# Two banks for the transposed weights, both heads' weights-times-v in one two-bank tile, and a new order of a pair's steps

## The chip, the cores and the metric

The kernel runs on one core of one Trainium2 chip. The metric is device microseconds from start to end of the program. TensorE (PE) does the matrix products and the transposes, VectorE (DVE), ScalarE (ACT) and GpSimd (POOL) the elementwise work, and the SP queue issues the transfers.

## The reference, cut to what matters

B = 2, H = 8, S = 576, D = 64. For each of the 16 heads a causal attention is mixed with a read-out of a memory, and the result (1152 tokens x 512) goes through two dense layers.

```
scores = scale * q @ k.T ; causal mask ; a = softmax(scores) ; local = a @ v
q_p = phi(q)                                  # elu(q) + 1
mem_out = (q_p @ M_prev) / (q_p @ z_prev + 1e-6)
x = g * mem_out + (1 - g) * local             # g from beta, one per head
h = ((x @ w1) * (x @ w2)) @ w3 ; x2 = h @ w_out
out = sum over 4 experts of p_e * (relu(x2 @ w1[e]) @ w2[e])
```

## The kernel before, in words

All products are taken in single precision; a value is split into a high and a low part where a product is done in three passes (`PASSES`).

**Slots.** The two heads of a pair share the 128 partitions. There are 8 pairs, and a loop of nine slots (n = -1 to 7, `run_slot`, L338). Slot n holds, for pair n, stage b (transposes of the weights, products with v, memory read-out, joining, `stage_b`, L242); for pair n+1, phi and stage a (scores and exponentials, L198); for pair n+2, the split of q and k (`stage_h`, L158). Besides this come "fill" steps that belong to the dense layers: folding w3 and w_out into one matrix W in slots 0 to 3 (L394), the a and b products of the first batch in slots 4 to 6.4 (L446), and the product with W from 6.4 to 8 (L507). Each step has a number between 0 and 1, its place in the slot (`H_AT`, `PHI_AT`, `A_AT`, `B_AT`, and `B_STEP` = 0.48 added for the odd head); the fill steps are spread evenly; the program writes all of them down in the order of these numbers. After slot 7 come the second batch and the four experts.

**Order on the engines.** The framework's planner takes the written order as priority, and lets an instruction of lower priority go first on an engine where by its model the one before it is not ready. The resulting order of each engine is fixed before the run: every engine takes its instructions in that order and waits at the head of its queue.

**Stage b before.** A head's 15 blocks of weights are transposed in groups of 4, 4, 4 and 3 (`trans`, L254) into the one bank of `psT`, and ACT copies each group to the tile pT in SBUF (L263). A product with v (`pv`, L266) goes into the one bank of `psQ`, head by head. `mem` (L279) takes one of the two two-bank tiles of `psS` for both heads. `join` (L303) divides a head's result on DVE (L306, L309, L311) and adds the memory part on POOL (L312). `fin` (L314) transposes the pair's result (L325) into a `psS` tile, whence ACT and DVE write xT (L328, L82). The scores of stage a (L212) also use the `psS` tiles, four times a pair. With `psM` (two banks) all eight banks are in use: 2 + 4 + 1 + 1.

In slot n the even head's steps lie at 0.02 to 0.42 and the odd head's at 0.50 to 0.90, in turn with the fill steps: transposes, then products with v that need their copies, then more transposes.

Of the kernel before, what the change touches and what calls it, by code (L numbers as in the profile page):

```python
# [8 lines left out]
F32 = mybir.dt.float32  # L9
# [4 lines left out]
ALU = mybir.AluOpType  # L14
AX = mybir.AxisListType
PSUM = bass.MemoryType.PSUM


H_AT = (0.6, 0.7, 0.62, 0.72)
PHI_AT = (0.3, 0.4)  # L20
A_AT = (0.25, 0.34, 0.43, 0.52)
B_AT = (0.02, 0.07, 0.1, 0.12, 0.15, 0.17, 0.22, 0.27, 0.32, 0.34, 0.42)
B_STEP = 0.48

WO_SLOTS = (-0.9, -0.8, -0.7, -0.6, -0.3, -0.1, 0.1, 0.2)
W_SLOTS, B_SLOTS, C_SLOTS = (0.0, 4.0), (4.0, 6.4), (6.4, 8.0)
# [7 lines left out]
def kernel(  # L34
# [17 lines left out]
    nc = tc.nc  # L52
    B, H, D, S = qT.shape
# [4 lines left out]
    P = 128  # L58
    KD = DM // P
    KF = DF // P  # L60
    NQ = 5
    RP = 120
# [9 lines left out]
    def r32(ap):  # L72
        return ap.bitcast(F32)
# [7 lines left out]
    def lo_dve(dst, src, hi):  # L81
        nc.vector.tensor_sub(dst, src, r32(hi))  # L82

    main = ctx.enter_context(tc.tile_pool(name="main", bufs=1, side="left"))
    gm = main.tile([P, H], F32, name="gm")
    gl = main.tile([P, H], F32, name="gl")
# [6 lines left out]
    def from64(raw, tmp, nm):  # L93
# [21 lines left out]
    attn = ExitStack()  # L115
    A1 = attn.enter_context(tc.tile_pool(name="A1", bufs=1, side="right"))
    A2 = attn.enter_context(tc.tile_pool(name="A2", bufs=2, side="right"))
# [7 lines left out]
        out=mask[:, S0:], in_=mask[:, S0:], compare_op=ALU.is_ge, fill=-MASK,  # L125
        base=0, pattern=[[-1, RP]], channel_multiplier=1,
    )
    psS = attn.enter_context(tc.tile_pool(name="psS", bufs=2, space=PSUM))
    psQ = attn.enter_context(tc.tile_pool(name="psQ", bufs=1, space=PSUM))
    psT = attn.enter_context(tc.tile_pool(name="psT", bufs=1, space=PSUM))  # L130


    raw_t, qk_t, phi_t, prob_t, xq_t, xm_t = {}, {}, {}, {}, {}, {}

    mz = A1.tile([P, B * H // 2, D + 1], F32, name="mz")

    v4 = [A1.tile([RP, NQ, D + 1], F32, name=f"v{i}") for i in range(4)]
# [20 lines left out]
    def stage_h(p):  # L158

        if p >= B * H // 2:  # L160
            return []
        qd, kd = raw_t[p]
        qk_t[p] = [A1.tile([P, 2, S], F32R, tag=f"{x}s", name=f"{x}s{p}") for x in "qk"]
        qs, ks = qk_t[p]
        return [
            *zip(
                H_AT,
                (
                    lambda: nc.scalar.copy(qs[:, 0, :], qd),
                    lambda: nc.scalar.copy(ks[:, 0, :], kd),  # L170
                    lambda: lo_pool(qs[:, 1, :], qd, qs[:, 0, :]),
                    lambda: lo_pool(ks[:, 1, :], kd, ks[:, 0, :]),
                ),
            )
        ]

    def stage_phi(p):
# [13 lines left out]

        return [*zip(PHI_AT, (f0, f1))]

    q0 = [R * i for i in range(NQ)]
    widths = [x + RP for x in q0]
    rows = [R] * (NQ - 1) + [RP]

    def stage_a(p):  # L198
# [37 lines left out]
        )  # L236
        return [(at, lambda c=c: scores(*c)) for at, c in zip(A_AT, steps)]

    NB = 4
    blocks = [(i, j) for i in range(NQ) for j in range(i + 1)]  # L240

    def stage_b(n):  # L242


        b, h = divmod(n, H)
        p, o = n // 2, n % 2 * D
        Pt, vn, phi = prob_t.pop(n), v4[n % 4], phi_t[p]
        st = {}
        pt = {}
        if n % 2 == 0:  # L250
            xq_t[0] = A2.tile([RP, NQ, 2, D], F32, tag="xq", name=f"xq{p}")
        xq = xq_t[0]

        def trans(g):  # L254
            def f():
                mine = blocks[g * NB : (g + 1) * NB]
                ps = psT.tile([P, 512], F32, tag="T", name=f"pt{g}_{n}")[0:RP, 0 : RP * len(mine)]
                t = A2.tile([RP, RP * len(mine)], F32, tag=f"pt{g}", name=f"pT{g}_{n}")
                for x, (i, j) in enumerate(mine):
                    sl = slice(x * RP, (x + 1) * RP)  # L260
                    nc.tensor.transpose(ps[:, sl], Pt[i][:, q0[j] : q0[j] + RP], identF[0:RP, 0:RP])  # L261
                    pt[i, j] = t[:, sl]
                nc.scalar.copy(t, ps)  # L263
            return f

        def pv(*tiles):  # L266
            def f():
                if "a" not in st:
                    ps = psQ.tile([P, 512], F32, tag="Q", name=f"a{n}")[0:RP, 0 : NQ * (D + 1)]
                    st["a"] = ps.rearrange("p (i d) -> p i d", d=D + 1)  # L270
                for i in tiles:
                    for j in range(i + 1):
                        nc.tensor.matmul(  # L273
                            st["a"][:, i, :], lhsT=pt[i, j][0 : rows[j]], rhs=vn[0 : rows[j], j, :],
                            start=(j == 0), stop=(j == i),
                        )
            return f

        def mem():  # L279
            if n % 2 == 1:  # L280
                return
            ps = psS.tile([P, 2, 512], F32, tag="S", name=f"b{p}")[0:RP, :, 0 : NQ * (D + 1)]
            m = ps.rearrange("p x (i d) -> p x i d", d=D + 1)
            for i in range(NQ):
                for x in range(2):
                    o = slice(x * D, (x + 1) * D)
                    nc.tensor.matmul(
                        m[:, x, i, :], lhsT=phi[o, q0[i] : q0[i] + RP], rhs=mz[o, p, :], start=True, stop=True
                    )
            r2 = A2.tile([RP, 2, NQ], F32, tag="rm", name=f"rm{p}")  # L290
            for x in range(2):
                nc.vector.tensor_scalar(
                    out=r2[:, x, :], in0=m[:, x, :, D], scalar1=1e-6, scalar2=gm[0:RP, h + x : h + x + 1],
                    op0=ALU.add, op1=ALU.mult,
                )
            nc.vector.reciprocal(r2, r2)
            xm_t[0] = dst = A2.tile([RP, 2, NQ, D], F32, tag="xm", name=f"xm{p}", bufs=1)
            for x in range(2):
                nc.vector.tensor_mul(
                    dst[:, x], m[:, x, :, 0:D], r2[:, x, :].unsqueeze(2).to_broadcast([RP, NQ, D])  # L300
                )

        def join():  # L303
            a = st["a"]
            rr = A2.tile([RP, NQ], F32, tag="rr", name=f"rr{n}")
            nc.vector.tensor_scalar(  # L306
                out=rr, in0=a[:, :, D], scalar1=1e-9, scalar2=gl[0:RP, h : h + 1], op0=ALU.add, op1=ALU.mult
            )
            nc.vector.reciprocal(rr, rr)  # L309
            xh = xq[:, :, n % 2, :]  # L310
            nc.vector.tensor_mul(xh, a[:, :, 0:D], rr.unsqueeze(2).to_broadcast([RP, NQ, D]))  # L311
            nc.gpsimd.tensor_add(xh, xh, xm_t[0][:, n % 2])  # L312

        def fin():  # L314
            if n % 2 == 0:
                return
            if b:
                xT[b, h // 2] = main.tile([P, 2, S], F32R, tag=f"g{p}", name=f"xT{b}_{h // 2}")
            xt = xT[b, h // 2]

            o0 = 512 - q0[NQ - 1]
            ps = psS.tile([P, 1024], F32, tag="S", name=f"x{p}")[:, o0 : o0 + S]
            for c in range(NQ):
                w = rows[c]
                nc.tensor.transpose(  # L325
                    ps[:, q0[c] : q0[c] + w], xq[0:w, c].rearrange("p h d -> p (h d)"), identF[0:w, 0:w]
                )
            nc.scalar.copy(xt[:, 0, :], ps)  # L328
            lo_dve(xt[:, 1, :], ps, xt[:, 0, :])

        return [
            *zip(
                [x + n % 2 * B_STEP for x in B_AT],
                (trans(0), trans(1), mem, trans(2), pv(0, 1), trans(3), pv(2), pv(3), pv(4), join, fin),
            )
        ]

    def run_slot(n, fill):  # L338
        steps = stage_h(n + 2) + stage_phi(n + 1) + stage_a(n + 1)
        steps += stage_b(2 * n) + stage_b(2 * n + 1) if n >= 0 else []  # L340
        steps += [((i + 0.5) / len(fill), f) for i, f in enumerate(fill)]
        for _, f in sorted(steps, key=lambda t: t[0]):
            f()
# [260 lines left out]
    for e in range(E):  # L604
        nxt = None
        for c, (c0, cw) in enumerate(CHUNKS):
            hs = []
            for m in range(KF):
                ps = ps3.tile([P, 512], F32, tag="P", name=f"d{e}_{c}_{m}")[:, 0:cw]
                n = 0  # L610
                for kk in range(KD):
                    rhs = x2a[kk][:, :, c0 : c0 + cw] if c0 < CA else x2b[kk][:, :, c0 - CA : c0 - CA + cw]
                    for wi, xi in PASSES:
                        nc.tensor.matmul(  # L614
                            ps, lhsT=ew1[m // 4 * 4 + kk][:, wi, m % 4 * P : (m % 4 + 1) * P],
                            rhs=rhs[:, xi, :], start=(n == 0), stop=(n == 3 * KD - 1),
# [5 lines left out]
                    out=ht[:, 1, :], in0=ps, scalar=0.0, in1=r32(ht[:, 0, :]),  # L622
                    op0=ALU.max, op1=ALU.subtract,
                )
                hs.append(ht)
            for tt in range(cw // P):
                po = ps3.tile([P, 512], F32, tag="P", name=f"o{e}_{c}_{tt}")
                n = 0
                for kk in range(KF):
                    for xi, wi in PASSES:  # L630
                        nc.tensor.matmul(  # L631
                            po, lhsT=hs[kk][:, xi, tt * P : (tt + 1) * P], rhs=ew2[kk][:, wi, :],
# [55 lines left out]
```

## Time and profile before

| | |
|---|---|
| three runs | 790.2, 799.09 and 799.87 us; median 799.09 us |
| the profiled execution | 802.59 us, its span 800.8 us, so 1.8 us lie around the span |
| busy: PE, DVE, ACT, POOL | 760.1 us (95%), 305.3 (38%), 255.5 (32%), 249.2 (31%) |
| mean granted TensorE clock | 0.972 |
| attention and fill (slots) | from 0 to about 312 us; the second batch and the experts follow |

A row of the chronological view gives the start, the duration, the engine, the source line, the operation, the tile written and the tiles read, how many instructions are merged in the row, and in brackets how long the engine stood idle before it and what ended that. A product with v and one of mem count as two PE instructions in the trace, a transpose as one. A granted clock of 1.00 is 2.4 GHz, 0.50 is 1.2 GHz.

### The profile page before, as it was taken

To read this page: it belongs to the slowest core of one execution; us is meant where nothing else is said; L and a number is where in the kernel's file an instruction comes from. 1 tells how busy PE (TensorE), PEld (TensorE's weight loads), DVE (VectorE), ACT (ScalarE), POOL (GpSimd) and SP (SyncE) were. 2 spreads that over 40 slices of the span, in tenths; PEclk is the share of its full clock that TensorE was granted. 3 is DMA by queue.
4 is the path that set the end of the run, shared out by engine and by line. 5 is a ranking of instruction groups with operands and counts; after the bars stand their busy time and mean duration, and the time that the engine had idled before them with its cause. 6 is when DMAs were issued, how large, how long until landed. Compare 5 with 4: busy or idle time off the path is not lost.

```text
span 800.8 us, 11325 instructions
## 1 busy us (share of the span) xinstructions
PE 760.1 (95%) x4568; PEld 671.9 (84%) x4568; DVE 305.3 (38%) x650; ACT 255.5 (32%) x503; POOL 249.2 (31%) x252
## 2 busy tenths in 40 slices
PE   4889999899999998899999999999999999999998
PEld 2668778799988898889988988889888898888986
DVE  7965574537676421655331211212112121121211
ACT  7855564636565522455220101201012010120100
POOL 2253544215453103923392009500085001600000
PEclk9989999859999998999999999999999999999999
DMA  9753303302423001541141004200033000201010
GB/s 270 270 170 102 117 17 91 91 19 79 141 84 114 28 1 53 158 145 54 29 131 53 0 1 121 90 1 0 1 118 94 1 0 1 67 1 39 14 40 27
DMA packets 52596, 56.69 MB, mean 71 GB/s; under 512 B 15552, under 2 KB 40128, under 8 KB 52544
## 3 DMA queue, kind: packets, MB, share of 16 engines
q1 hardware_dynamic: 52544, 55.97, 23.2%
q8 instruction: 36, 0.59, 0.3%
q14 instruction: 16, 0.13, 0.1%
HBM read 53.60 MB, written 2.36 MB: 70 GB/s over the span
## 4 chain that ended last, share of the span: by engine, by line
PE 58%; POOL 3%; issue 2%; DMA 1%; DVE 1%; ACT 1%; POOLq 0%; SPq 0%; DVEq 0%; ACTq 0%
PE d L614 25%; PE o L631 25%; PE c L507 4%; PE ab L446 3%; POOL el L79 1%; DMA wr<-in_moe_w_dram 1%; POOL ws L79 1%; POOL el L76 1%; PE a L273 1%; PE pt L261 0%; ACT tu L101 0%; POOL xq L312 0%; DVE P L224 0%; DVE tu L103 0%; PE x L325 0%
## 5 line engine op out<-in xcount | busy, mean ns | idle before, releaser
L631 PE MATMUL o<-el,he 128*128 128x512 f32 x864 | 201.3, 393 | 0.0
L631 PEld LDWEIGHTS o<-el,he 128*128 128x128 f32 x864 | 161.8, 188 | 36.5
L620 ACT ACTIVATE he<-d 128x512 fp32r<-128x512 f32 (+2 forms) x96 | 47.2, 491 | 342.4 <-PE d L614 339.9
L446 PE MATMUL ab<-xT,ws 128*128 128x288 f32 x768 | 120.7, 309 | 4.1 <-DVE asb L494 1.7
L446 PEld LDWEIGHTS ab<-xT,ws 128*128 128x128 f32 x768 | 110.0, 197 | 7.8 <-issue 2.9
L614 PE MATMUL d<-x2b,el 128*128 128x384 f32 (+1 forms) x768 | 113.7, 308 | 0.0
L614 PEld LDWEIGHTS d<-x2b,el 128*128 128x128 f32 x768 | 113.1, 189 | 0.7
L621 DVE SCALAR_TENSOR_TENSOR he<-d,he 128x512 fp32r<-128x512 f32 (+2 forms) x96 | 53.6, 558 | 147.8 <-ACT he L620 147.8
L76 POOL TENSOR_SCALAR el<-rel 128x512 fp32r<-128x512 f32 x64 | 40.4, 637 | 213.7 <-PE d L614 186.2
L614 PE MATMUL d<-x2a,el 128*128 128x512 f32 x384 | 89.6, 394 | 0.0
L614 PEld LDWEIGHTS d<-x2a,el 128*128 128x128 f32 x384 | 72.0, 188 | 16.8
L79 POOL TENSOR_TENSOR el<-rel,el 128x512 fp32r<-128x512 f32 x64 | 83.6, 1322 | 1.6
L640 DVE SCALAR_TENSOR_TENSOR acc<-o,pr,acc 128x512 f32<-128x512 f32 x27 | 20.3, 751 | 125.7 <-PE o L631 125.7
L273 PE MATMUL a<-v,pT 114*120 114x65 f32 (+1 forms) x480 | 66.4, 284 | 0.1
L273 PEld LDWEIGHTS a<-v,pT 114*120 114x120 f32 (+1 forms) x480 | 63.8, 206 | 2.4 <-ACT tu_l L101 0.7
L507 PE MATMUL c<-hT,W 128*128 128x288 f32 x384 | 58.5, 300 | 3.3 <-DVE hT L82 3.0
L394 PE MATMUL wacc<-wo,w3s 128*128 128x512 f32 x192 | 56.0, 442 | 3.0 <-DVE W L82 2.4
L507 PEld LDWEIGHTS c<-hT,W 128*128 128x128 f32 x384 | 52.3, 188 | 5.6 <-DVE hT L82 3.1
L79 POOL TENSOR_TENSOR ws<-tf,ws 128x512 fp32r<-128x512 f32 x32 | 43.3, 1354 | 40.5 <-ACT ws L436 35.5
L261 PE MATMUL pt<-identF,P 120*120 120x120 f32 x240 | 41.3, 295 | 11.7 <-ACT pT L263 9.8
L394 PEld LDWEIGHTS wacc<-wo,w3s 128*128 128x128 f32 x192 | 39.6, 214 | 12.5 <-issue 3.3
L218 PE MATMUL sc<-ks,qs 64*120 64x120 f32 (+5 forms) x288 | 36.8, 381 | 12.4 <-POOL ks L79 8.6
(75 smaller groups left out, 654.8 us busy)
## 6 DMA issues: line engine op xcount, KB each, us to landing
wr<-in_moe_w_dram SPq DMA_DIRECT2D x32, 512.0 KB, 3.6
rel<-in_moe_w_dram SPq DMA_DIRECT2D x64, 256.0 KB, 2.7
w3r<-in_moe_w3T_dram SPq DMA_DIRECT2D x16, 512.0 KB, 3.7
wor<-in_moe_w_out_dram SPq DMA_DIRECT2D x8, 512.0 KB, 7.0
v<-in_v_dram SPq DMA_DIRECT2D x16, 150.0 KB, 3.9
qd<-in_qT_dram SPq DMA_DIRECT2D x8, 288.0 KB, 4.1
kd<-in_kT_dram SPq DMA_DIRECT2D x8, 288.0 KB, 3.9
out_dram<-acc SPq DMA_DIRECT2D x9, 256.0 KB, 2.0
```

What stands on the lines that cost most here:

```text
L76: nc.gpsimd.tensor_scalar(out=dst, in0=src, scalar1=1.0, scalar2=1.0, op0=ALU.mult, op1=ALU.mult)
L79: nc.gpsimd.tensor_sub(dst, src, r32(hi))
L218: nc.tensor.matmul(ps[x][:, c : c + k1 - k0], lhsT=qs[o, a, q0[i] : q0[i] + RP], rhs=ks[o, b, k0:k1], start=(m == 0), stop=(m == 2),)
L261: nc.tensor.transpose(ps[:, sl], Pt[i][:, q0[j] : q0[j] + RP], identF[0:RP, 0:RP])
L273: nc.tensor.matmul(st["a"][:, i, :], lhsT=pt[i, j][0 : rows[j]], rhs=vn[0 : rows[j], j, :], start=(j == 0), stop=(j == i),)
L394: nc.tensor.matmul(wacc[t], lhsT=w3s[u][:, a, c, :], rhs=wo[4 * g + c][:, bb, :], start=(g == 0 and c == 0 and x == 0), stop=(g == 1 and c ...
L446: nc.tensor.matmul(ps[:, 0:HS], lhsT=self.ws[u][:, wi, kk, :], rhs=xT[b, kk][:, xi, a * HS : (a + 1) * HS], start=(n == 0), stop=(n == 3 * ...
L507: nc.tensor.matmul(st["ps"][:, 0:HS], lhsT=Wt[kk][:, wi, d * P : (d + 1) * P], rhs=hT[kk][:, xi, a * HS : (a + 1) * HS], start=(kk == 0 an ...
L614: nc.tensor.matmul(ps, lhsT=ew1[m // 4 * 4 + kk][:, wi, m % 4 * P : (m % 4 + 1) * P], rhs=rhs[:, xi, :], start=(n == 0), stop=(n == 3 * KD ...
L620: nc.scalar.activation(ht[:, 0, :], ps, AF.Relu)
L621: nc.vector.scalar_tensor_tensor(out=ht[:, 1, :], in0=ps, scalar=0.0, in1=r32(ht[:, 0, :]), op0=ALU.max, op1=ALU.subtract,)
L631: nc.tensor.matmul(po, lhsT=hs[kk][:, xi, tt * P : (tt + 1) * P], rhs=ew2[kk][:, wi, :], start=(n == 0), stop=(n == 3 * KF - 1),)
```

## The change

`psQ` is dropped and `psT` gets two banks. `stage_b` is called once per pair. The eight groups of transposes (four per head) are written at 0.01 to 0.29 (`T_AT`); the products with v of head 0 at 0.40 and of head 1 at 0.48 go into the two banks of one `psS` tile; `join` at 0.54 divides both heads (two divisors, one reciprocal, two products on DVE) and adds the memory part in one POOL instruction of twice the length; `fin` is at 0.68 (before 0.90). The scores move from 0.25, 0.34, 0.43, 0.52 to 0.20, 0.27, 0.34, 0.41; the split of q and k from 0.60 to 0.72 to 0.50 to 0.62; phi from 0.30 and 0.40 to 0.60 and 0.70; `mem` from 0.10 to 0.11. The memory part is kept with the two heads side by side (`xm` is [120, 5, 2, 64] in place of [120, 2, 5, 64]).

```
-H_AT = (0.6, 0.7, 0.62, 0.72)
-PHI_AT = (0.3, 0.4)
-A_AT = (0.25, 0.34, 0.43, 0.52)
-B_AT = (0.02, 0.07, 0.1, 0.12, 0.15, 0.17, 0.22, 0.27, 0.32, 0.34, 0.42)
-B_STEP = 0.48
+H_AT = (0.5, 0.6, 0.52, 0.62)
+PHI_AT = (0.6, 0.7)
+A_AT = (0.2, 0.27, 0.34, 0.41)
+T_AT = (0.01, 0.05, 0.09, 0.13, 0.17, 0.21, 0.25, 0.29)
+MEM_AT, PV_AT, JOIN_AT, FIN_AT = 0.11, (0.4, 0.48), 0.54, 0.68
...
-    psQ = attn.enter_context(tc.tile_pool(name="psQ", bufs=1, space=PSUM))
-    psT = attn.enter_context(tc.tile_pool(name="psT", bufs=1, space=PSUM))
+    psT = attn.enter_context(tc.tile_pool(name="psT", bufs=2, space=PSUM))
...
+        def pv(x):
             def f():
-                if "a" not in st:
-                    ps = psQ.tile([P, 512], F32, tag="Q", name=f"a{n}")[0:RP, 0 : NQ * (D + 1)]
-                    st["a"] = ps.rearrange("p (i d) -> p i d", d=D + 1)
-                for i in tiles:
+                vn = v4[(2 * p + x) % 4]
+                if x == 0:
+                    ps = psS.tile([P, 2, 512], F32, tag="S", name=f"a{p}")[0:RP, :, 0 : NQ * (D + 1)]
+                    st["a"] = ps.rearrange("p x (i d) -> p x i d", d=D + 1)
+                for i in range(NQ):
...
+        def scaled(dst, ps, eps, gate, nm):
+
+            r = A2.tile([RP, 2, NQ], F32, tag=f"r{nm}", name=f"r{nm}{p}")
+            for x in range(2):
+                nc.vector.tensor_scalar(
+                    out=r[:, x, :], in0=ps[:, x, :, D], scalar1=eps, scalar2=gate[0:RP, h + x : h + x + 1],
+                    op0=ALU.add, op1=ALU.mult,
+                )
+            nc.vector.reciprocal(r, r)
+            for x in range(2):
+                nc.vector.tensor_mul(dst(x), ps[:, x, :, 0:D], r[:, x, :].unsqueeze(2).to_broadcast([RP, NQ, D]))
...
         def join():
...
+            scaled(lambda x: xq[:, :, x, :], st["a"], 1e-9, gl, "a")
+            nc.gpsimd.tensor_add(xq, xq, st["m"])
...
         return [
-            *zip(
-                [x + n % 2 * B_STEP for x in B_AT],
-                (trans(0), trans(1), mem, trans(2), pv(0, 1), trans(3), pv(2), pv(3), pv(4), join, fin),
-            )
+            *zip(T_AT, (trans(x, g) for x in range(2) for g in range(4))),
+            (MEM_AT, mem), (PV_AT[0], pv(0)), (PV_AT[1], pv(1)), (JOIN_AT, join), (FIN_AT, fin),
         ]
...
-        steps += stage_b(2 * n) + stage_b(2 * n + 1) if n >= 0 else []
+        steps += stage_b(n) if n >= 0 else []
```

## Rows read from the trace of the kernel before

**Rows 1.** The page: busy time of each engine, and PE and the granted clock in 40 slices of 20 us (tenths).
```profile
PE 760.1 (95%) x4568; PEld 671.9 (84%) x4568; DVE 305.3 (38%) x650; ACT 255.5 (32%) x503; POOL 249.2 (31%) x252
...
PE   4889999899999998899999999999999999999998
...
PEclk9989999859999998999999999999999999999999
```

**Rows 2.** Busy time by stage (start:end, length, then busy us and count of PE, PE weight loads, DVE, ACT, POOL, then granted clock, DMA share, GB/s): the start, the slots to 180 us, the later slots.
```profile
8.60:41.00 32.40, 25.23 (x140) 20.04 (x141) 30.92 (x79) 26.88 (x52) 4.98 (x4) 1.00 0.92 277
41.00:180.00 139.00, 128.85 (x821) 110.03 (x819) 75.87 (x194) 73.56 (x136) 55.19 (x53) 0.86 0.29 85
180.00:308.00 128.00, 124.52 (x1031) 117.46 (x1031) 69.93 (x171) 65.09 (x131) 42.19 (x39) 1.00 0.23 70
```

**Rows 3.** Who PE waited for from 41 to 312 us: us in total, times, longest.
```profile
PE pt L261 <- ACT pT L263: 8.7, 8, 3.4
PE wacc L394 <- DVE W L82: 2.4, 2, 2.2
PE x L325 <- POOL xq L312: 2.0, 1, 2.0
```

**Rows 4.** PE and ACT in order of time, from 152 to 163 us.
```profile
152.81 0.63 PE L261 MATMUL pt<-identF,P 120*120 120x120 f32 x4 [0.90 <-ACT pT L263]
...
153.28 0.96 PE L273 MATMUL a<-v,pT 114*120 114x65 f32 x8
153.54 0.68 ACT L101 ACTIVATE tu<-wr 128x512 uint32<-128x512 uint16 x1 [0.78 <-DMA wr<-in_moe_w_dram]
154.13 0.76 ACT L231 ACTIVATE P<-P,mn 120x576 f32<-120x576 f32 x1
...
154.79 0.54 ACT L263 COPY pT<-pt 120x480 f32<-120x480 f32 x1
...
155.38 0.85 PE L261 MATMUL pt<-identF,P 120*120 120x120 f32 x3 [1.15 <-ACT pT L263]
...
160.45 1.05 PE L261 MATMUL pt<-identF,P 120*120 120x120 f32 x4 [0.70 <-ACT pT L263]
...
161.29 1.72 PE L273 MATMUL a<-v,pT 114*120 114x65 f32 x8
```

**Rows 5.** Busy time and granted clock in slices of 5 us (columns as in rows 2) around it.
```profile
150.00:155.00 5.00, 3.28 (x27) 2.77 (x26) 2.08 (x7) 4.22 (x8) 3.59 (x3) 0.99 0.48 131
155.00:160.00 5.00, 4.36 (x21) 3.98 (x21) 0.91 (x3) 0.95 (x3) 0.00 (x0) 0.50 0.31 93
170.00:175.00 5.00, 5.00 (x29) 4.66 (x29) 1.83 (x9) 2.75 (x7) 1.89 (x2) 0.50 0.00 0
```

**Rows 6.** Work on PE in order of time: products of W, transposes, and a and b products, at the low and at the full clock.
```profile
56.13 5.87 PE L394 MATMUL wacc<-wo,w3s 128*128 128x512 f32 x18
...
82.24 4.39 PE L394 MATMUL wacc<-wo,w3s 128*128 128x512 f32 x18
...
89.11 0.57 PE L261 MATMUL pt<-identF,P 120*120 120x120 f32 x4
...
121.15 4.65 PE L394 MATMUL wacc<-wo,w3s 128*128 128x512 f32 x13 [2.17 <-DVE W L82]
...
173.74 5.71 PE L446 MATMUL ab<-xT,ws 128*128 128x288 f32 x24
...
180.88 3.45 PE L446 MATMUL ab<-xT,ws 128*128 128x288 f32 x24
```

**Rows 7.** ACT and PE in order of time, from 52 to 54 us.
```profile
52.16 0.67 ACT L102 ACTIVATE tf_l<-w3r 128x512 f32<-128x512 f32 x1 [2.59 <-POOL w3s L79]
...
53.20 0.56 ACT L263 COPY pT<-pt 120x480 f32<-120x480 f32 x1
53.81 1.06 PE L261 MATMUL pt<-identF,P 120*120 120x120 f32 x4 [3.45 <-ACT pT L263]
```

**Rows 8.** The end of the slots in order of time, all engines.
```profile
308.44 0.22 DVE L306 TENSOR_SCALAR rr<-a,gl 120x5 f32<-120x5 f32 x1 [3.25 <-PE a L273]
...
309.50 0.86 POOL L312 TENSOR_TENSOR xq<-xq,xm 120x320 f32<-120x320 f32 x1 [12.11 <-DVE xq L311]
...
310.41 0.71 PE L325 MATMUL x<-identF,xq 114*128 114x114 f32 x5 [2.00 <-POOL xq L312]
...
312.64 8.64 PE L446 MATMUL ab<-xT,ws 128*128 128x288 f32 x42 [1.52 <-DVE xT L82]
```

**Rows 9.** Costliest groups (line, engine, tiles, shapes, count | busy us, mean ns | idle before): the instructions that the change touches.
```profile
L263 ACT COPY pT<-pt 120x480 f32<-120x480 f32 x64 | 33.7, 527 | 38.2 <-PE pt L261 38.2
L224 DVE CUSTOM_DVE_ANT_0 P<-sc,mask,mn 120x512 f32<-120x512 f32 x16 | 11.4, 745 | 0.0
L312 POOL TENSOR_TENSOR xq<-xq,xm 120x320 f32<-120x320 f32 x16 | 15.6, 976 | 68.8 <-DVE xq L311 68.7
L311 DVE TENSOR_TENSOR xq<-a,rr 120x320 f32<-120x320 f32 x16 | 7.8, 488 | 0.3
L306 DVE TENSOR_SCALAR rr<-a,gl 120x5 f32<-120x5 f32 x16 | 3.5, 221 | 19.7 <-PE a L273 19.5
L309 DVE RECIPROCAL rr<-rr 120x5 f32<-120x5 f32 x16 | 3.0, 188 | 0.4
L296 DVE RECIPROCAL rm<-rm 120x10 f32<-120x10 f32 x8 | 1.7, 209 | 0.0
```

More of the change, by code (lines that the diff above doesn't have):

```diff
@@ L128 @@
     psS = attn.enter_context(tc.tile_pool(name="psS", bufs=2, space=PSUM))
-    psQ = attn.enter_context(tc.tile_pool(name="psQ", bufs=1, space=PSUM))
-    psT = attn.enter_context(tc.tile_pool(name="psT", bufs=1, space=PSUM))
-    raw_t, qk_t, phi_t, prob_t, xq_t, xm_t = {}, {}, {}, {}, {}, {}
+    psT = attn.enter_context(tc.tile_pool(name="psT", bufs=2, space=PSUM))
+    raw_t, qk_t, phi_t, prob_t = {}, {}, {}, {}
     mz = A1.tile([P, B * H // 2, D + 1], F32, name="mz")
@@ L240, with stage_b, trans @@
     blocks = [(i, j) for i in range(NQ) for j in range(i + 1)]
[L242 to L254, printed above, removed]
+    def stage_b(p):
+        b, h = divmod(2 * p, H)
+        phi = phi_t[p]
+        pt, st = {}, {}
+        xq = A2.tile([RP, NQ, 2, D], F32, tag="xq", name=f"xq{p}")
+        def trans(x, g):
@@ L255, in f @@
             def f():
+                Pt = prob_t[2 * p + x]
                 mine = blocks[g * NB : (g + 1) * NB]
[L257 to L260, printed above, removed]
+                ps = psT.tile([P, 512], F32, tag="T", name=f"pt{g}_{2 * p + x}")[0:RP, 0 : RP * len(mine)]
@@ L261, in f @@
+                t = A2.tile([RP, RP * len(mine)], F32, tag=f"pt{g}", name=f"pT{g}_{2 * p + x}")
+                for y, (i, j) in enumerate(mine):
+                    sl = slice(y * RP, (y + 1) * RP)
                     nc.tensor.transpose(ps[:, sl], Pt[i][:, q0[j] : q0[j] + RP], identF[0:RP, 0:RP])
-                    pt[i, j] = t[:, sl]
+                    pt[x, i, j] = t[:, sl]
                 nc.scalar.copy(t, ps)
             return f
-        def pv(*tiles):
+        def pv(x):
             def f():
-                if "a" not in st:
-                    ps = psQ.tile([P, 512], F32, tag="Q", name=f"a{n}")[0:RP, 0 : NQ * (D + 1)]
-                    st["a"] = ps.rearrange("p (i d) -> p i d", d=D + 1)
-                for i in tiles:
+                vn = v4[(2 * p + x) % 4]
[3 more added lines that the diff above has]
+                for i in range(NQ):
@@ L272, in f @@
                     for j in range(i + 1):
                         nc.tensor.matmul(
-                            st["a"][:, i, :], lhsT=pt[i, j][0 : rows[j]], rhs=vn[0 : rows[j], j, :],
+                            st["a"][:, x, i, :], lhsT=pt[x, i, j][0 : rows[j]], rhs=vn[0 : rows[j], j, :],
                             start=(j == 0), stop=(j == i),
@@ L277, in pv @@
             return f
+        def scaled(dst, ps, eps, gate, nm):
[8 more added lines that the diff above has]
+                nc.vector.tensor_mul(dst(x), ps[:, x, :, 0:D], r[:, x, :].unsqueeze(2).to_broadcast([RP, NQ, D]))
         def mem():
-            if n % 2 == 1:
-                return
             ps = psS.tile([P, 2, 512], F32, tag="S", name=f"b{p}")[0:RP, :, 0 : NQ * (D + 1)]
@@ L289, in mem @@
                     )
[L290 to L294, printed above, removed]
-                )
[L296 to L301, printed above, removed]
-        def join():
[L304 to L312, printed above, removed]
+            st["m"] = A2.tile([RP, NQ, 2, D], F32, tag="xm", name=f"xm{p}", bufs=1)
+            scaled(lambda x: st["m"][:, :, x, :], m, 1e-6, gm, "m")
+        def join():
+            scaled(lambda x: xq[:, :, x, :], st["a"], 1e-9, gl, "a")
+            nc.gpsimd.tensor_add(xq, xq, st["m"])
         def fin():
-            if n % 2 == 0:
-                return
             if b:
@@ L331, in stage_b @@
         return [
-            *zip(
-                [x + n % 2 * B_STEP for x in B_AT],
-                (trans(0), trans(1), mem, trans(2), pv(0, 1), trans(3), pv(2), pv(3), pv(4), join, fin),
-            )
+            *zip(T_AT, (trans(x, g) for x in range(2) for g in range(4))),
+            (MEM_AT, mem), (PV_AT[0], pv(0)), (PV_AT[1], pv(1)), (JOIN_AT, join), (FIN_AT, fin),
         ]
```

## The prediction

> **What bounds the kernel now.** I read the page first. PE is busy for 760.1 of 800.8 us, the other engines for 31 to 38%; in the 40 slices PE's idle time and its low clocks lie in the first 16, which are the attention slots and the change-over [rows 1]. From 400 us on PE runs without a gap at the full clock; nothing of the change is there. The busy time by stage parts the slots in three [rows 2]. To 41 us DVE is the busiest engine (30.92 of 32.40 us), with conversions and the first scores; the change takes none of that work away. From 41 to 180 us PE idles for 139.00 - 128.85 = 10.2 us and has a mean clock of 0.86. From 180 to 308 us it idles for only 3.5 us, at 1.00. So there is something to win from 41 to 180 us and at the end of the slots, and little elsewhere.
>
> The waits say for whom PE idles: of what is listed from 41 to 312 us, 8.7 us go to transposes that wait for the ACT copy of the group before, because there is one bank for it, 2.4 us to the copy of W, 2.0 us to the last pair's POOL addition [rows 3]. The chronological view shows the mechanism: transposes at 152.81, 155.38 and 160.45 us each wait for a copy, and the copy ahead of 155.38 us stood in ACT's queue behind a conversion that waited for a DMA and behind an exponential [rows 4]; at 53.81 us the wait is 3.45 us because ACT stood still for 2.59 us for POOL [rows 7]. Behind such stalls the clock falls: to 0.50 from 155 us on, and though PE is then busy for 4.36 to 5.00 of every 5 us, it stays there until the a and b products of 173.74 us [rows 5, 6].
>
> **What a low clock costs, from rows.** 24 a and b products take 5.71 against 3.45 us, eight products with v 1.72 against 0.96, four transposes 1.05 against 0.57 [rows 4, 6]: the full clock needs about 0.57 of the time (mean of 0.60, 0.56 and 0.54). The long stretch runs from 155.38 to 173.74 + 5.71 = 179.45 us, less 0.70 of idle time: 23.4 us, of which 43% is 10 us. After 53.81 us: 18 products of W in 5.87 against 4.39 us, so 1.5, and the 2.3 us ahead of them another 1.0: 2.5. After 121.15 us: 13 of them in 4.65 where 13 x 4.39 / 18 = 3.17 would do: 1.5 [rows 6]. After the slots: 42 products in 8.64 where 42 x 3.45 / 24 = 6.04 would do: 2.6 [rows 6, 8].
>
> **The change part by part.**
>
> *Second transpose bank, and transposes well ahead of the products with v.* A group now waits for the copy of the group before last, and the products with v stand some steps behind it, so a late copy has time. Bounds: 0 (ACT is as late as before and only the waiter changes) to 8.7 us [rows 3]. A second bank buys one group, 0.57 us, plus what the order puts between; seven of the eight waits have 5.3 us together and should mostly vanish, the 3.45 us one only in half: I take 6.
>
> *The clock behind these stalls.* Bounds 0 to 10 + 2.5 us. If the long stretch doesn't begin, its 10 us are won whole; the groups at 53.81 us start at the low clock if any real gap is left. I take 9. The 1.5 us after 121.15 us stay, since that wait is for the copy of W, which the change doesn't touch.
>
> *fin at 0.68 in place of 0.90.* In slot 7 the chain from the last product with v over DVE, POOL, PE, ACT and DVE has nothing behind it: 2.00 + 1.52 us idle and 2.6 us of low clock, 6.1 us [rows 8]. With `fin` at 0.68 some third of the slot's fill steps remain behind it: of 20 steps of six products at 0.144 us [rows 6] six, 5 us, and more before it since `pv` ends at 0.48. The new join is longer: on DVE two divisors, one reciprocal, two products, 2 x 0.221 + 0.209 + 2 x 0.488 = 1.63 us, on POOL at most twice 0.976 [rows 9]; 3.6 us, which the fill covers. Bounds 0 to 6.1; I take 5.
>
> *Join once a pair.* DVE goes from 16 x (0.221 + 0.188 + 0.488) = 14.4 to 8 x 1.63 = 13.0 us, POOL from 15.6 to at most 15.6 [rows 9]. DVE is busy for 55% from 41 to 308 us, so this is worth 0 on the path; without that cover the lower bound is a loss of 8 x 0.98 = 8 us, if every `fin` waited for the longer POOL addition. `fin` stands 0.14 of a slot (some 4 us, with 8 slots in about 270 us) behind `join`, so 0.
>
> *psS now serves seven uses a pair, not six, and one is held from the first product with v to the end of `join`.* Scores come at steps of 0.07 in place of 0.09 of a slot, 2.4 us. A score step is reduced by DVE in at most 2 x 0.745 us [rows 9]; while `pv` holds one tile, the last score step (0.41) needs the tile of the third (0.34). Bounds: 0 to one whole reduction a pair, 8 x 1.5 = 12 us. No row from 41 to 312 us shows scores waiting [rows 3], and fill can go first, so nearer the low end: 3 us lost.
>
> *Moves of `stage_h`, phi, `mem`, scores.* Splits write q and k after the last score step, as before (0.09 of a slot behind, before 0.08). phi now ends at 0.70, and `mem` needs it at 1.11, 0.4 of a slot later. SP: the next load of q is held until phi at 0.70 has read it, and the loads of v and of weights queue behind it on SP; that load is written at 1.0, so it doesn't wait. Nothing, with a bound of one load's lateness. ACT: the 8 copies of 0.527 us [rows 9] are now in 0.01 to 0.29, ahead of the exponentials; the same work.
>
> *Sum* against the profiled execution: 802.6 - 6 - 9 - 5 + 3 = 785.6 us. That execution is 3.5 us above the median of 799.1, and one of the three runs is at 790.2, a distance about that of one long stretch at the low clock; so part of the 9 us may be won already in some runs of the kernel before. I forecast **784 us**, 1.9% under the median; between 772 and 796 for this case.
>
> **A rule against the change.** The trace shows the low clock staying on through 155 to 175 us while PE did transposes, products with v and `mem` at 87 to 100% busy [rows 4, 5]. The new order packs a pair's transposes together. The Trainium skill, "TensorE: Matmul & The Clock Gate", section "Part 4: PE-mode transpose", says that the full rate does not engage for transposes done on TensorE. The trace agrees only for that stretch: four transposes took 0.57 us at the full clock at 89.11 us, between other products [rows 6]. That is rival 4.
>
> **The rivals.**
> 1. *More goes than I take*: all 8.7 us, the 12.5 us of clock behind them and 6.1 us at the end: 802.6 - 27.3 = 775, and 770 if the W waits and their clock go too. For it: these lines hang together, a stall and then a clock. Against: ACT is still one queue. Chance 0.15.
> 2. *The waits change their name.* ACT stays late behind conversions, the products with v or the scores wait in place of the transposes, or the planner puts the transposes where they stood; only the end of the slots is won, 5 us: 797 from the profile, 794 from the median, and 788 to 802 with one long stretch more or less. For it: the 3.45 us wait began at POOL, not in the bank [rows 7]. Chance 0.24.
> 3. *Slower: psS.* The two-bank tile is held over `pv`, `join` and what the planner puts between, and the scores wait at its other tile. 8 x 1.5 us, and two new stretches at the low clock of 10 us each, on what is won at the end: 802.6 + 12 + 20 - 5 = 830; with one stretch 820. It decides from about 3 us of wait a pair. Against: fill can go first. Chance 0.07.
> 4. *Slower: the clock.* A pair's attention work (30 transposes, 60 instructions of products with v) runs at the low clock in most slots: per pair 7.5 x 0.48 + 7.5 x 0.76 = 9.3 us [rows 4, 6]; for half of the six pairs from 41 to 308 us, 28 us: 802.6 - 11 + 28 = 820. Against: half the fill steps stand between. Chance 0.06.
>
> **How the numbers follow.** Forecast 0.48. A measurement of this kernel can tell about 2% from no change, so faster means under 783.1 us and slower over 815.1. Faster: somewhat under half of the forecast's case (0.22), nearly all of rival 1 (0.14), little of rival 2 (0.02): 0.38. Slower: most of rivals 3 and 4: 0.11. The rest, 0.51, is within 2%. The range goes from 768 (most of rival 1) to 808 (all of rival 2, the weak forms of 3 and 4).
>
> **What would show it.** Right: transposes waiting for pT copies at under 3 us in all; no stretch of 20 us at 0.50 between 41 and 308 us; transposes of the last pair followed by products c, with x in the last slot behind no wait over 0.5 us and the first a and b products of the second batch at 0.144 us. DVE busy 1 to 2 us less, POOL equal. Wrong: score, v or memory products that wait for DVE by more than 5 us in all (rival 3), the granted clock under 0.86 from 41 to 180 us without stalls (rival 4), waits for pT copies moved to the products with v (rival 2).

## The result, and the profile after

The changed kernel takes 771.85 us (median of 4 executions, 771.13 to 772.93), the kernel before 794.64 us in the same set (789.97 to 799.87): a ratio of 0.9713, 95% interval 0.963 to 0.9795. Two of the four executions before lie at 790 us and two at 799 to 800, so 794.64 is a value between two groups; the three sets of experiments below have medians of 798 to 800 us for the same kernel. The profiled execution took 772.15 us, its span is 770.4 us. The first product of the experts starts at 365.61 us, before at 396.04: the whole gain lies in front of it.

The page: busy time of each engine, PE and the granted clock in 40 slices (of 19.3 us).
```profile
PE 743.0 (96%) x4568; PEld 656.0 (85%) x4568; DVE 299.5 (39%) x642; ACT 252.6 (33%) x503; POOL 246.1 (32%) x244
...
PE   4899999999999998999999999999999999999997
...
PEclk9999999999999999999999999999999999999999
```
Against [rows 1]: the spans differ by 30.4 us. PE's busy time fell by 17.1 us with the same 4568 instructions, so that part is speed, the clock; its idle time fell from 40.7 to 27.4 us, 13.3 us. No slice is below 9 tenths of the clock now.

Busy time by stage, columns as in [rows 2], and two slices of 5 us as in [rows 5].
```profile
8.60:41.00 32.40, 26.69 (x147) 21.58 (x147) 31.04 (x83) 29.66 (x58) 4.98 (x4) 1.00 0.89 272
41.00:180.00 139.00, 138.35 (x1028) 118.63 (x1029) 89.91 (x221) 84.16 (x161) 68.57 (x61) 1.00 0.35 102
180.00:308.00 128.00, 120.80 (x965) 113.98 (x964) 64.61 (x150) 60.18 (x127) 49.16 (x43) 1.00 0.28 85
...
120.00:125.00 5.00, 5.00 (x43) 3.87 (x41) 3.60 (x18) 4.29 (x10) 0.76 (x1) 1.00 0.05 10
...
155.00:160.00 5.00, 5.00 (x45) 5.00 (x43) 3.63 (x14) 3.16 (x7) 1.86 (x2) 1.00 0.06 17
```
From 41 to 180 us PE idles for 0.65 us where it idled for 10.2, at a mean clock of 1.00 where it was 0.86. It starts 1028 instructions there, before 821. From 180 to 308 us it idles more than before, 7.2 us against 3.5. But the slots end at 283.14 us now and ended at 312.64 before: 4.8 of the 7.2 us lie in the slots and 2.4 in the second batch, which the stretch holds only of the changed kernel. From the end of the slots to the experts PE idles for 3.7 us now and for 4.0 before.

Who PE waited for from 41 to 312 us, all rows, and then a row of the kernel before that [rows 3] leaves out.
```profile
PE ab L432 <- DVE asb L480: 3.2, 4, 1.8
PE ab L432 <- POOL ks L79: 1.9, 1, 1.9
PE ab L432 <- POOL ws L79: 1.7, 1, 1.7
PE sc L217 <- DVE mn L223: 0.6, 1, 0.6
PE ab L432 <- ACT asb L440: 0.3, 1, 0.3
PE pt L257 <- ACT pT L259: 0.3, 1, 0.3
PE c L493 <- DVE hT L82: 0.2, 1, 0.2
```
```profile
PE ab L446 <- DVE asb L494: 1.0, 2, 0.9
```
Transposes wait for copies for 0.3 us in place of 8.7, and the waits for W and for the last xq are gone [rows 3]. The a and b products wait longer: 3.2 us for DVE in place of 1.0, and 3.6 us for POOL, where before they waited for none. Of these, 0.9 and 1.7 us lie behind 283 us, in the second batch.

PE in order of time: a pair's transposes, products with v and products of W; then the end of the slots, which answers to [rows 8].
```profile
52.83 0.98 PE L257 MATMUL pt<-identF,P 120*120 120x120 f32 x8
54.13 0.99 PE L257 MATMUL pt<-identF,P 120*120 120x120 f32 x7 [0.32 <-ACT pT L259]
54.88 5.72 PE L380 MATMUL wacc<-wo,w3s 128*128 128x512 f32 x24
60.44 0.37 PE L257 MATMUL pt<-identF,P 120*120 120x120 f32 x2
60.64 0.66 PE L313 MATMUL x<-identF,xq 114*128 114x114 f32 x5
61.23 1.26 PE L294 MATMUL b<-mz,phi 64*120 64x65 f32 x20
62.43 0.83 PE L257 MATMUL pt<-identF,P 120*120 120x120 f32 x6
63.02 3.68 PE L380 MATMUL wacc<-wo,w3s 128*128 128x512 f32 x15
...
99.69 3.48 PE L270 MATMUL a<-v,pT 114*120 114x65 f32 x32
...
280.78 0.66 PE L313 MATMUL x<-identF,xq 114*128 114x114 f32 x5
281.20 2.10 PE L493 MATMUL c<-hT,W 128*128 128x288 f32 x14
283.14 6.65 PE L432 MATMUL ab<-xT,ws 128*128 128x288 f32 x49
```
Two groups of transposes now run together (eight in 0.98 us), the products with v come later in one block of a head, and 24 products of W, one tile of W, take 5.72 us, the full clock's pace (18 in 4.39 us in [rows 6]). While that tile is copied out, PE does transposes, `fin` and `mem` from 60.44 to 63.02 us. At the end the last `fin` waits for nothing, products c follow it, and 49 a and b products take 0.136 us each; before, the same place lost 3.5 us idle and ran 42 products in 8.64 us [rows 8].

The costliest groups: the products with v on PE, and `join`'s addition and product, as in [rows 9].
```profile
L270 PE MATMUL a<-v,pT 114*120 114x65 f32 (+1 forms) x480 | 56.7, 276 | 0.4 <-DVE mn L223 0.4
L302 POOL TENSOR_TENSOR xq<-xq,xm 120x640 f32<-120x640 f32 x8 | 12.5, 1564 | 37.7 <-DVE xq L286 37.7
L286 DVE TENSOR_TENSOR xq<-a,ra 120x320 f32<-120x320 f32 x16 | 7.1, 486 | 0.3
```

### The profile page after: what moved, and what is told of

It reads as the page before. It is cut to its first block, busy times and chain, and to the rows that moved or that the text cites. A ratio compares the mean times of both kernels' runs of the same rounds, so it can differ in the third digit from the quotient of the medians.

```text
span 770.4 us, 11304 instructions
## 1 busy us (share of the span) xinstructions
PE 743.0 (96%) x4568; PEld 656.0 (85%) x4568; DVE 299.5 (39%) x642; ACT 252.6 (33%) x503; POOL 246.1 (32%) x244
## 4 chain that ended last, share of the span: by engine, by line
PE 63%; DMA 2%; DVE 1%; POOL 1%; ACT 1%; issue 0%; DVEq 0%; SPq 0%; ACTq 0%
PE d L600 26%; PE o L617 26%; PE c L493 6%; PE ab L432 3%; DMA wr<-in_moe_w_dram 2%; PE a L270 1%; DVE tu L103 0%; POOL ws L79 0%; DVE tf L106 0%; PE pt L257 0%; POOL el L76 0%; POOL el L79 0%; DVE hT L82 0%; ACT tu L101 0%; ACT tf L102 0%
## 5 line engine op out<-in xcount | busy, mean ns | idle before, releaser
L432 PE MATMUL ab<-xT,ws 128*128 128x288 f32 x768 | 113.1, 299 | 7.2 <-DVE asb L480 3.2
L432 PEld LDWEIGHTS ab<-xT,ws 128*128 128x128 f32 x768 | 103.9, 188 | 10.2 <-DVE asb L480 3.3
L270 PEld LDWEIGHTS a<-v,pT 114*120 114x120 f32 (+1 forms) x480 | 55.4, 193 | 3.9 <-issue 2.6
L270 PE MATMUL a<-v,pT 114*120 114x65 f32 (+1 forms) x480 | 56.7, 276 | 0.4 <-DVE mn L223 0.4
L79 POOL TENSOR_TENSOR ws<-tf,ws 128x512 fp32r<-128x512 f32 x32 | 44.9, 1402 | 38.2 <-ACT ws L422 36.9
L380 PE MATMUL wacc<-wo,w3s 128*128 128x512 f32 x192 | 49.9, 408 | 0.0
L217 PE MATMUL sc<-ks,qs 64*120 64x120 f32 (+5 forms) x288 | 37.2, 375 | 12.5 <-POOL ks L79 9.3
L230 ACT ACTIVATE P<-P,mn 120x120 f32<-120x120 f32 (+3 forms) x80 | 42.4, 578 | 2.0 <-DVE mn L223 1.8
L380 PEld LDWEIGHTS wacc<-wo,w3s 128*128 128x128 f32 x192 | 35.9, 194 | 7.6 <-issue 0.7
```

The lines of the kernel that those rows point to most:

```text
L79: nc.gpsimd.tensor_sub(dst, src, r32(hi))
L217: nc.tensor.matmul(ps[x][:, c : c + k1 - k0], lhsT=qs[o, a, q0[i] : q0[i] + RP], rhs=ks[o, b, k0:k1], start=(m == 0), stop=(m == 2),)
L230: nc.scalar.activation(Pt[i], Pt[i], AF.Exp, bias=mn[:, i : i + 1], scale=-1.0)
L270: nc.tensor.matmul(st["a"][:, x, i, :], lhsT=pt[x, i, j][0 : rows[j]], rhs=vn[0 : rows[j], j, :], start=(j == 0), stop=(j == i),)
L380: nc.tensor.matmul(wacc[t], lhsT=w3s[u][:, a, c, :], rhs=wo[4 * g + c][:, bb, :], start=(g == 0 and c == 0 and x == 0), stop=(g == 1 and c ...
L432: nc.tensor.matmul(ps[:, 0:HS], lhsT=self.ws[u][:, wi, kk, :], rhs=xT[b, kk][:, xi, a * HS : (a + 1) * HS], start=(n == 0), stop=(n == 3 * ...
```

## The experiments

Two theories stood against each other: **BANK**, that the second transpose bank is what frees PE, and **PLACES**, that the new order of the steps is. "Before" in the sets below is the kernel before, run on the same chip beside each set. The changed kernel itself is not in these sets; where a run is compared with its 771.85 us, the two come from different sets.

**1. One transpose bank in the changed kernel.**
```
-    psT = attn.enter_context(tc.tile_pool(name="psT", bufs=2, space=PSUM))
+    psT = attn.enter_context(tc.tile_pool(name="psT", bufs=1, space=PSUM))
```


> The changed kernel with one psT bank in place of two (the eighth bank stays empty); places and the common psS tile are kept. Theory BANK (the second bank lets PE go on while ACT copies): waits of transposes for pT copies return to 6 to 9 us, a stretch at the low clock returns, 785 to 795 us. Theory PLACES (the transposes stand far ahead of the products with v, and other work stands between them): pT waits stay under 3 us, no long stretch at the low clock, 770 to 777 us.

Measured: 794.77 us (788.99 to 802.47, 10 executions), ratio to before 0.9988 (0.994 to 1.0035). The whole gain is gone. Its profile is of the fastest execution (788.99 us); its waits of PE from 41 to 312 us, and then its stage up to 180 us:
```profile
PE pt L257 <- ACT pT L259: 7.4, 7, 3.0
PE wacc L380 <- DVE W L82: 1.6, 2, 0.9
...
PE a L270 <- ACT pT L259: 1.2, 1, 1.2
```
```profile
41.00:180.00 139.00, 127.62 (x902) 107.41 (x902) 82.21 (x204) 79.58 (x150) 61.03 (x53) 0.98 0.32 93
```
BANK: the waits for copies are back (7.4 us), those for W with them, and PE idles for 11.4 us from 41 to 180 us. This execution had a mean clock of 0.995, and what it loses is mostly idle time: over the whole span PE idles for 39.6 us (27.4 in the changed kernel) and is busy for 747.6 us (743.0). The other nine ran at clocks of 0.979 to 0.989. The written places are the same, but the order on PE is not: with one bank the planner puts other work between the groups, and no more than four transposes stand in a row, where the changed kernel has up to eight. So what the bank is worth includes the order that the planner makes of it.

**2. The steps at their places of before, with the changed kernel's banks.**
```
-H_AT = (0.5, 0.6, 0.52, 0.62)
-PHI_AT = (0.6, 0.7)
-A_AT = (0.2, 0.27, 0.34, 0.41)
-T_AT = (0.01, 0.05, 0.09, 0.13, 0.17, 0.21, 0.25, 0.29)
-MEM_AT, PV_AT, JOIN_AT, FIN_AT = 0.11, (0.4, 0.48), 0.54, 0.68
+H_AT = (0.6, 0.7, 0.62, 0.72)
+PHI_AT = (0.3, 0.4)
+A_AT = (0.25, 0.34, 0.43, 0.52)
+T_AT = (0.02, 0.07, 0.12, 0.17, 0.5, 0.55, 0.6, 0.65)
+MEM_AT, PV_AT, JOIN_AT, FIN_AT = 0.1, (0.15, 0.22, 0.27, 0.32, 0.63, 0.7, 0.75, 0.8), 0.82, 0.9
...
+            *zip(PV_AT, (pv(x, *t) for x in range(2) for t in ((0, 1), (2,), (3,), (4,)))),
```


> The changed kernel's banks (two for transposes, both heads' products with v in one psS tile) with every step at its place of before; join comes once, at 0.82, so the psS tile is held from 0.15 to 0.82 of the slot. BANK: the pT waits stay under 3 us; the time is 772 to 782 us unless the long hold costs. PLACES: products with v wait for copies in place of the transposes, 788 to 800 us. If the long hold of the psS tile costs what I feared, scores wait for DVE (mn, xq) by over 5 us and the time is above 795 us.

Measured: 778.51 us (777.93 to 779.49), ratio 0.9797 (0.9717 to 0.9876). Waits of PE from 41 to 312 us:
```profile
PE ab L433 <- DVE asb L481: 3.9, 3, 2.1
PE sc L217 <- DVE mn L223: 3.5, 3, 1.3
PE pt L257 <- ACT pT L259: 2.0, 3, 1.2
```
Most of the gain is here without any new place: BANK again. The long hold of the psS tile shows as scores that wait for DVE, 3.5 us, under the 5 us that I had set for it; the time stays 6.7 us above the changed kernel. That is idle time alone: PE is busy for 742.1 us, against 743.0.

**3. The new places with the banks of before.**
```
+H_AT = (0.5, 0.6, 0.52, 0.62)
+PHI_AT = (0.6, 0.7)
+A_AT = (0.2, 0.27, 0.34, 0.41)
+B_AT = (
+    (0.01, 0.05, 0.11, 0.09, 0.4, 0.13, 0.4, 0.4, 0.4, 0.46, 0.68),
+    (0.17, 0.21, 0.11, 0.25, 0.48, 0.29, 0.48, 0.48, 0.48, 0.54, 0.68),
+)
...
-                [x + n % 2 * B_STEP for x in B_AT],
+                B_AT[n % 2],
```


> The kernel before with its banks (one for transposes, one psQ for one head's products with v) and the steps at the changed kernel's places; join of head 0 at 0.46, of head 1 at 0.54. BANK: pT waits 6 to 9 us, 788 to 798 us. PLACES: under 3 us, 770 to 778 us; head 1's products wait for head 0's join in psQ by at most 0.6 us a pair, 5 us in all.

Measured: 786.03 us (784.28 to 787.62), ratio 0.9889 (0.9821 to 0.9956), between the two expectations. Waits of PE from 41 to 312 us:
```profile
PE pt L263 <- ACT pT L265: 4.3, 4, 2.8
PE ab L448 <- ACT asb L456: 3.0, 1, 3.0
PE a L275 <- ACT pT L265: 1.6, 3, 0.7
```
The places alone halve the transposes' waits, though products with v now wait for copies for 1.6 us, and give some 12 us; in the changed kernel they add 6.7 us to what the banks give (run 2). Neither theory alone is the whole; the bank is the larger part. Run 1 has these places and one bank too and is 8.7 us slower than run 3: with one transpose bank, the common psS tile and the `join` once a pair together made things worse. In the two profiles, 2.6 us apart, PE idles from 8.6 to 180 us for 32.4 - 23.0 + 11.4 = 20.8 us in run 1 and 32.4 - 25.5 + 7.9 = 14.8 us in run 3. Which of the two causes that is open.

**4. `fin` late.** `FIN_AT` 0.90 in place of 0.68, nothing else.

> The changed kernel with fin at 0.90 in place of 0.68, nothing else. My term for the end of the slots: 3.5 us of idle time and some 2.6 us of low clock return at the change-over, 776 to 779 us. Rival: with the products with v already at 0.48 the chain behind them is covered anyway, and the time stays within 771 to 774 us.

Measured: 772.69 us (771.66 to 773.32); the changed kernel had 771.13 to 772.93. The written place of `fin` is worth nothing. Its end of the slots, and then that of run 2:
```profile
271.00 3.26 PE L270 MATMUL a<-v,pT 114*120 114x65 f32 x30
274.08 6.60 PE L493 MATMUL c<-hT,W 128*128 128x288 f32 x48
280.52 0.66 PE L313 MATMUL x<-identF,xq 114*128 114x114 f32 x5
280.94 1.84 PE L493 MATMUL c<-hT,W 128*128 128x288 f32 x12
```
```profile
283.89 3.44 PE L494 MATMUL c<-hT,W 128*128 128x288 f32 x24
...
288.37 0.66 PE L313 MATMUL x<-identF,xq 114*128 114x114 f32 x5
...
290.55 4.73 PE L433 MATMUL ab<-xT,ws 128*128 128x288 f32 x31 [0.32 <-DVE xT L82]
```
The last products with v end at 271.00 + 3.26 us, and 48 products c cover the whole chain to `fin`. The planner put `fin` at 280.52 us, in the changed kernel at 280.78, so the other number hardly moved it on PE. Nor is it the early place of the products with v: in run 2, where they and `fin` are written at their places of before, PE waits for 0.32 us in all there, behind 24 products c and some a and b products. What matters is that work is left for PE behind the last products with v. Before, none was left [rows 8].

**5. The kernel before once more**, for a second profile.

> The kernel before, unchanged, for a second profile. If the differences between its executions (790 to 804 us) are stretches at the low clock, as I read its first trace, this profile's waits of PE agree with the first one's within 2 us in all, while its low-clock stretches differ, and the span follows the mean granted clock: about 788 us at 0.985, 796 at 0.978. If stalls differ instead, the waits differ by as much as the span.

Measured: 806.35 us, mean clock 0.967. Its waits from 41 to 312 us, and then two slices of 5 us:
```profile
PE pt L261 <- ACT pT L263: 9.7, 7, 3.4
PE wacc L394 <- DVE W L82: 2.4, 2, 2.2
```
```profile
170.00:175.00 5.00, 5.00 (x29) 4.79 (x30) 1.83 (x9) 2.75 (x7) 1.89 (x2) 0.50 0.00 0
255.00:260.00 5.00, 5.00 (x38) 4.61 (x37) 4.37 (x16) 2.76 (x7) 0.56 (x1) 0.69 0.20 47
```
The waits are the first profile's within 1 us each, the stretch from 155 to 175 us is there again, and a further one at 255 us that the first profile doesn't have: there, at 254.73 us, a group of transposes waited for its copy for 1.55 us, in the first profile for 0.33. Over the executions of the kernel before in the three sets, time follows the mean granted clock:
```
us      788.98 790.19 794.77 797.69 798.16 799.83 800.97
clock    0.989  0.987  0.982  0.978  0.976  0.974  0.974
```
Seven are shown, of the twenty executions up to 800.97 us. A straight line through the twenty gives 7.0 us for each 0.01 of clock, with a scatter of 1.3 us about it, and 782 us at a clock of 1.00, which is extrapolated from 0.993; with the seven slower executions (to 804.01 us) it is 7.3 us and 782. The second profile at 0.967 lies on the line too (805 us). An estimate from the prediction's figures agrees: 0.01 less of mean clock is 16 of 800 us spent at 0.50, and 43% of that is 6.9 us. So nearly all of the spread is work done at the low clock; as the place at 254.73 us shows, a wait that is 1.2 us longer in one execution can stand at the start of it. By the line, some 16 of the 26 us from the twenty's median of 798 us to the changed kernel are clock, and some 10 are idle time.

**6. Scores, phi and split at their places of before.**
```
-H_AT = (0.5, 0.6, 0.52, 0.62)
-PHI_AT = (0.6, 0.7)
-A_AT = (0.2, 0.27, 0.34, 0.41)
+H_AT = (0.6, 0.7, 0.62, 0.72)
+PHI_AT = (0.3, 0.4)
+A_AT = (0.25, 0.34, 0.43, 0.52)
```


> The changed kernel with scores, phi and the split of q and k at their places of before (scores 0.25, 0.34, 0.43, 0.52; phi 0.30, 0.40; split 0.60 to 0.72); transposes, products with v, join and fin stay at the new ones. If the 7 us that the new places are worth with two banks come from the distance between transposes and products with v: 770 to 775 us. If they come from the scores and phi being earlier: 777 to 780 us.

Measured: 771.21 us (770.51 to 771.82), ratio to before 0.968 (0.9599 to 0.9761). These moves are worth nothing, if anything they cost 0.6 us. So what the places are worth lies with those of the transposes, the products with v and `join`; only that of the products with v was tried by itself (run 7).

**7. Products with v right behind their transposes.** `PV_AT` (0.15, 0.31) in place of (0.4, 0.48), `join` still at 0.54.

> The changed kernel with the products with v right behind their head's transposes, at 0.15 and 0.31 in place of 0.40 and 0.48; join stays at 0.54, so the psS tile is held through three score steps. If the distance matters: products with v wait for pT copies by 3 to 8 us, 777 to 790 us. My rival on psS: scores wait for DVE at the other tile by 5 to 12 us in all, 780 to 795 us. If neither matters: 770 to 774 us.

Measured: 775.53 us (774.28 to 776.73), 3.7 us above the changed kernel. Waits from 41 to 312 us:
```profile
PE a L270 <- ACT pT L259: 1.1, 2, 0.6
...
PE sc L217 <- DVE mn L223: 0.5, 1, 0.5
```
The distance is worth something, less than I set, and products with v wait for copies for only 1.1 us. The psS tile is held through three score steps, and scores wait for 0.5 us, products of `mem` for another 0.5: the rival on psS falls.

**8 and 9. The pT copy done twice**, in the kernel before and in the changed one.
```
                 nc.scalar.copy(t, ps)
+                nc.scalar.copy(t, ps)
```


> The kernel before with every pT copy on ACT done twice (64 more ACT copies of 0.53 us, the same values written again), so that a transpose group's bank is held 0.5 us longer. Theory BANK: with one bank each group waits longer; the waits for pT copies go from 9 us to 15 us or more, the low-clock stretches grow, and the time rises by 8 to 30 us over the kernel before. Rival (ACT's load, not the bank, is what PE waits for): the rise is the same in both kernels of this pair.

> The changed kernel with the same doubling. Theory BANK: two banks and the distance to the products with v hide it; waits for pT copies stay under 3 us and the time rises by at most 4 us, to 772 to 776 us. Rival: it rises as much as the other kernel of this pair does, 780 us or more.

Measured: 815.52 us (813.75 to 816.24; before in this set 798.89) and 775.09 us (774.73 to 775.76): 16.6 us more with one bank, 3.2 us more with two. First of 8, waits from 41 to 312 us and then the stage to 180 us:
```profile
PE pt L261 <- ACT pT L264: 9.0, 6, 4.3
PE wacc L395 <- DVE W L82: 3.1, 2, 2.6
```
```profile
41.00:180.00 139.00, 123.64 (x763) 104.18 (x761) 73.30 (x177) 83.27 (x156) 54.82 (x50) 0.84 0.28 85
```
and of 9, the stage alone (no row for pT copies is among its waits from 41 to 312 us):
```profile
41.00:180.00 139.00, 134.63 (x976) 116.59 (x976) 85.55 (x219) 99.19 (x197) 66.42 (x59) 0.99 0.35 101
```
The times come out as BANK said. The pair compares the two whole kernels, so it does not tell the bank from the places; runs 1 to 3 do. The waits did not rise to 15 us in 8: with a longer copy in its model the planner places the work differently, and the loss shows as more idle time from 41 to 180 us (15.4 us against 10.2) and a lower clock (0.84).

**10. A try at the start: w_out's two parts on POOL** in the changed kernel.
```
-            nc.scalar.copy(wo[c][:, 0, :], f)
-            lo_dve(wo[c][:, 1, :], f, wo[c][:, 0, :])
+            hi_pool(wo[c][:, 0, :], f)
+            lo_pool(wo[c][:, 1, :], f, wo[c][:, 0, :])
```


> The changed kernel with the high and low parts of w_out taken on POOL in place of ACT and DVE, which are busy for 29.7 and 31.0 of the 32.4 us up to 41 us, while POOL is busy for 5.0. DVE loses 8 x 0.82 = 6.6 us, ACT 8 x 0.62 = 4.9 us there, POOL gains some 8 x 1.95 = 15.6 us. If the start is bound by DVE and ACT: 764 to 769 us. If it is bound by the loads of w3: 770 to 773 us. If POOL holds the split of q and k back: above 773 us.

Measured: 775.04 us (773.94 to 775.41), 3.2 us above the changed kernel. Its DVE groups from 8.6 to 41 us, and then the changed kernel's:
```profile
L103 DVE SCALAR_TENSOR_TENSOR tu_wo<-tf_wo,tu_wo 128x512 uint32<-128x512 uint32 x8 | 8.8, 1099 | 0.8 <-ACT tf_wo L102 0.8
```
```profile
L103 DVE SCALAR_TENSOR_TENSOR tu_wo<-tf_wo,tu_wo 128x512 uint32<-128x512 uint32 x8 | 5.4, 681 | 0.0
```
DVE lost eight instructions (6.9 us in that stage) and was still busy for 30.63 of 32.40 us, because those left became longer while POOL was busy: 1099 against 681 ns for the same operation. No run beats the changed kernel by more than run 6's 0.6 us.

## Why the prediction was right, and where its sizes were off

The forecast was faster, 784 us, 1.9% under the median; measured 771.85, within the range of 768 to 808. What came is what rival 1 described, 770 to 775 us, to which I gave 0.15. So the direction and the mechanism were right and the size was not: 771.85 lies just below the 772 to 796 of the forecast's own case, and by my chances a gain over 2% (0.38) was less likely than one within it (0.51).

- *Transposes waiting for copies:* right in kind. I took 6 of 8.7 us; 8.4 went. The 3.45 us wait, of which I kept half, went whole.
- *The clock behind the stalls:* **this is the mis-sized term.** I listed 10 + 2.5 us behind stalls of transposes, 1.5 after 121.15 us and 2.6 after the slots, 16.6 us in all; PE's busy time fell by 17.1 us, so all of it came. Of the 12.5 I took 9, and I kept the 1.5 us, "since that wait is for the copy of W, which the change doesn't touch". The waits for W vanished too, 2.4 us to none: while a tile of W is copied out, PE now has transposes that wait for no copy, `fin` and `mem` (60.44 to 63.02 us above), where it stood still for 2.17 us at 121.15 us [rows 6]. Run 1 brings those waits back (1.6 us) with one bank.
- *The end of the slots:* the 5 us came (no wait for xq or xT is left, no low clock at the change-over), but not through `fin` at 0.68: run 4 writes it at 0.90 at no loss, and run 2, with the steps at their places of before, loses only 0.32 us there. Products c are left behind the last products with v in both.
- *Join once a pair:* DVE is busy for 5.8 us less in all, where I had 1 to 2; of this, `join`'s operations are 2.7 us (11.6 in place of 14.3), and I had 1.4. POOL, which I had as equal, is busy for 3.1 us less, as one addition takes 1.564 us, not 2 x 0.976. No wait of PE in the view above is for either.
- *psS:* I took 3 us lost. Scores wait for 0.6 us; the seven uses fit, and run 7 holds the tile through three score steps at 0.5 us of waits. What I had not foreseen are the a and b products in the slots that wait behind DVE (2.3 us, before 1.0) and POOL (1.9, before none): PE reaches them before the product of the a and b results on DVE (L480) and the work on POOL are done.
- *Rival 2* (the waits change their name) is out: products with v wait for no copy. *Rival 3* (psS) falls with run 7, and in run 2 is worth 3.5 us. *Rival 4* (the clock falls under packed attention work) is out: the clock is 1.00 from 41 us on, through eight transposes in 0.98 us and 32 instructions of products with v in a row.

Added up, what the sum lacked is 2.4 us for transposes, 3.5 + 1.5 for the clock, 2.4 of waits for W, 1.1 at the end of the slots and 2.4 for psS: an estimate of 13.3 us, against 785.6 - 772.15 = 13.5. It leaves out the longer waits of a and b products in the slots, which go the other way.

By the row on rival 4, the statement of the Trainium skill ("TensorE: Matmul & The Clock Gate", section "Part 4: PE-mode transpose") that the full rate does not engage for transposes is not what this kernel shows: eight of them ran at the pace of the four at the full clock in [rows 6], 0.12 against 0.14 us each.

## What to carry to other kernels

Where TensorE fills one PSUM bank and waits for its copy, a small wait can be paid twice: once as idle time, once as the work behind it at the lower clock; here the second was the larger part (17.1 us of busy time against 13.3 idle). A second bank costs little if two results that are consumed together can share a tile that rotates anyway: scores waited for it for 0.6 us, and for 3.5 where it was held long (run 2). With two banks, writing the producing steps early and the consuming ones late gave another 6.7 us here; the places of `fin`, the scores and phi gave nothing. And judge a place by the order on the engine, not by the number written: the planner may leave the step where it was (run 4).

## What the runs showed of the hardware that was not expected

The spread of the kernel before, 789 to 801 us, is almost wholly told by one number, the mean granted clock (run 5): 7.0 us for each 0.01. A stretch of 20 us at 0.50 stands at the same place in both profiles, though PE was busy for 87 to 100% of each 5 us of it [rows 5]. It follows waits of 0.90 and 1.15 us (0.90 and 1.23 in the second profile); the third, of 0.70 us, fell when the clock was low already [rows 4]. In the changed kernel the executions lie within 1.8 us of each other, at clocks from 0.993 to 1.0.

A POOL addition of 120x640 takes 1.564 us by the profile. Two of 120x320 take 1.95 by their mean, but 11 of the 16 took 0.86 to 0.88 us and five 1.25 to 1.38: undisturbed, two take 1.74. DVE's two-input operations of 128x512 went from 681 to 1099 ns beside a POOL that was busy for 20.59 instead of 4.98 of 32.40 us. The Trainium skill, "SBUF — State Buffer", section "Who interferes with whom", says that a DVE instruction with two SBUF inputs contends with a GpSimd instruction that reads SBUF; run 10 agrees, and there it took back nearly all that the moved work had freed: DVE was busy for 30.63 us in place of 31.04. An operation with one input grew as well (L188 on `ex`, 450 to 735 ns), of which that sentence says nothing.
